# Moving a kernel's stores to a table among its score products, and two more warming products

## Chip, cores and metric

The kernel runs on one core of one Trainium2 chip. The metric is the device time of one execution in microseconds (us), the median of several runs. TensorE (PE) does the matrix products, VectorE (DVE), ScalarE (ACT) and GpSimd (POOL) the rest; SyncE (SP) issues most transfers, GpSimd the indirect ones.

## The reference, cut to what matters

```
scores = q @ k.T / 8                        # B = 8, H = 8, S = 576, D = 64, causal
scores += minimum(-(cum[i] - cum[j]), 0)    # cum: running sum of max(s, 0)
x[b, s, h*64:] = softmax(scores) @ v        # 4608 tokens of 512 numbers
logits = x @ w_gate                         # 8 experts
gate = sigmoid(x @ w_local)
e = argmax(logits) if first or gate < 0.5 else the expert of the token before
out = softmax(logits)[e] * (relu(x @ w1[e]) @ w2[e])
```

Everything is float32. A product in float32 is two records of each kind (weight load and product) in the trace.

## The kernel before, in words

**Attention.** The 64 heads are 32 pairs; the two heads of a pair use the two halves of TensorE's rows or columns at once. A *slot* m = 0 to 15 handles pairs n = 2m (even) and 2m + 1 (odd), and four slots' pairs cover two batch rows, a *group* g. In a slot TensorE first computes the score products of both pairs (`ps`, L874, 24 records a pair), in four units u = 0 to 3 for each pair. ACT exponentiates each unit into a tile e0 to e3 (L875), and POOL sets what lies above the diagonal to zero (the *masks*, L860: one each for e0, e1 and e2, two for e3). Then come the value products of the even pair and of the odd (`po`, L904, 100 records a pair), each in two parts of six and three blocks of 64 queries. The first blocks read the masked part of e0, the third block the masked part of e2, the fifth that of e3. DVE takes reciprocals (`recs`, L911) and writes the normalised tokens to `xb` (L912).

**Routing.** After each group the router computes logits of its 1152 tokens (`lp`, L216), the chosen experts, ranks within the expert (`pos`, L300 and L301), table rows (L309 to L316) and gates (up to L335). Then the group's tokens are stored to a `table` in DRAM, sorted by expert, in 18 stores of 64 tokens (128 half rows). One store (`put`) is two instructions on POOL, which runs its queue in order: a tiny write to `gap`, either a memset (L345) or a copy from a tile whose completion it thereby waits for (L347), and the indirect DMA (L348).

**Places.** The order on the engines is written out by hand. `plan(m, p, f)` puts work f at place p of slot m: 0 after the even pair's scores, 1 after the odd pair's, 3 and 4 after the even and odd values, 5 at the end of the slot. Since each engine takes its own instructions in this order, a store at place 0 stands on POOL behind the even pair's five masks, and one at place 1 behind the odd pair's. `STORES[g]` lists, from slot m + 2 on, the places at which a group's stores are issued; `m` is 4, 8 and 12. Stores at places 3, 4 and 5 copy an element of `recs`, so that they wait for the values named; the others don't wait. What `STORES` has no place for goes to `experts.puts`. The fourth group's stores all come later.

**Experts.** Tokens are handled in units of up to 256 rows of one expert. A unit's first layer is eight column blocks c = 0 to 7 (`hp`, L582, into `hT`, L584), its second layer `yp` (L606), whose result goes out by an indirect store (L611). In the first unit the loop takes one entry of `experts.puts` after each block, released by `hT` of that block; after block c = 2 the logits of the last group's second half are computed. When the list is empty in the first unit, rows of units 2 and 3 are fetched from the table by SP.

**Start.** Before the first score product TensorE multiplies zeros (`warm`, L809), while q and k arrive.

Of the kernel before, what the change touches and what calls it, by code (L numbers as in the profile page):

```python
# [45 lines left out]
NV = 4  # L46
NVA = 6
WEIGHED = (3, 7, 9, 11, 11, 13, 15, 19, 19, 21, 23, 27, 27, 30, 31, 31)
STORES = (((5,), (0, 1, 3, 4, 5), (0, 1, 3, 4, 5), (0, 1, 3, 4, 5), (0, 0)), ((5, 5), (0, 1, 3, 4, 5), (0, 1, 3, 4, 5), (0, 1, 1, 3, 4, 5)),
          ((5, 5), (0, 0, 1, 1, 3, 4, 5, 5)))  # L50
BX = 3
FIRST = ((0, P, 0, 3 * P), (P, S, 3 * P, S))
CAP = N + DH
# [399 lines left out]
class Experts:  # L453
# [165 lines left out]
    def run(self, recs, wend, out_of):  # L619
        tc, ctx, nc, router = self.tc, self.ctx, self.nc, self.router  # L620

        def pool(name, bufs, **kw):
            return ctx.enter_context(tc.tile_pool(name=name, bufs=bufs, reuse_waits="tile", **kw))

        self.w_rest = pool("w_rest", PLACES - 2)
        self.fp = pool("fp", 2)
        self.yp = pool("yp", 3)
        self.ps_h = pool("ps_h", 3, space=PSUM)
        self.ps_m = pool("ps_m2", 2, space=PSUM)
        self.ps_y = pool("ps_y", 2, space=PSUM)  # L630
        last, first = NG - 1, sum(EARLY)
        self.banks = lambda name: self.ps_m.tile([P, 1, 512], F32, name=name, tag="m")

        def late_rows():
            router.ranks(last, self.banks)
            router.rows(last)
            router.gates(last, self.xb)
            self.puts += [lambda after, c=c: router.scatter(last, c, after) for c in range(NC)]
            self.puts += router.pads()

        todo = {
            (0, 0): [lambda: self.load(0, 1, behind=self.hT[0][0:1, 0, 0:1]), lambda: self.load(1), lambda: router.assign_early(1), lambda: self.load(2)],
            (0, 2): [lambda: router.product(last, self.xts_of, self.banks, (1,)),
                     lambda: router.logits(last, (1,)), lambda: router.codes(last), lambda: router.exps(last),
                     lambda: router.turn1(last), lambda: router.turn2(last)],
            (0, "y"): [late_rows],
            (1, 2): [router.assign_doubles],
            (1, 5): [router.assign_rest],
            (2, 5): [lambda: in_range(tc, recs, wend, router.over, out_of, self.ps_m, router.ones)],
        }  # L650

        def at(u, c):
            for f in todo.pop((u, c), ()):
                f()

        before = {}
        for l in self.owner:
            for m in self.owner:
                if m < l and self.place(m) == self.place(l):
                    before[l] = m  # L660
        two = [m for m in self.owner if self.place(m) == "w_rest"]
        for i, l in enumerate(two):
            before[l] = two[i - 2] if i >= 2 else None
        self.turn_x(1)
        loaded, done, fetched, freed = [3, 3], (set(), set()), 2, False

        def ready(l, layer):
            nonlocal freed
            if before.get(l) is not None and self.owner[before[l]] not in done[layer]:
                return False  # L670
            if self.place(l) == "w_last" and not freed:
                if self.puts or todo:
                    return False
                self.x_stack.close()
                self.w_last = pool("w_last", 1, side="right")
                freed = True
            return True

        def loads():
            more = True  # L680
            while more:
                more = False
                for layer in range(2):
                    l = loaded[layer]
                    if l in self.owner and (not layer or l < loaded[0]) and ready(l, layer):
                        self.load(l, layer)
                        loaded[layer] += 1
                        more = True

        def fetches(u):  # L690
            nonlocal fetched
            while fetched <= u:
                self.fetch(fetched)
                fetched += 1

        def between(u):
            if self.puts:
                self.puts.pop(0)(None)
            at(u, "y")

        kinds = [k for k, _, _ in self.units]
        order = []
        u = 0
        while u < len(kinds):
            if u + 1 < len(kinds) and kinds[u + 1] in "MT":
                order += [(1, u), (1, u + 1), (2, u), (2, u + 1)]
                u += 2
            else:
                order += [(1, u), (2, u)]
                u += 1  # L710
        wanted = 0
        for what, u in order:
            last_wanted = wanted
            if what == 1:
                for c in range(FK):
                    self.layer1(u, c)
                    at(u, c)
                    if self.puts:
                        self.puts.pop(0)(self.hT[u][0:1, c, 0:1])
                    if u == 0 and fetched == 2 and not self.puts:  # L720
                        fetches(3)
                self.xT.pop(u)
                self.turn_h(u)
                if u:
                    self.turn_x(u + 1)
            else:
                self.layer2(u, lambda: between(u))
            done[what - 1].add(u)
            loads()
            if what == 1 and u and (u + 3 < first or not (self.puts or todo)):  # L730
                wanted = u + 3
            fetches(last_wanted)
        assert not todo and not self.puts


def attention(ctx, tc, q, k, v, s, wx, ident, recs, wend, router, experts):
# [69 lines left out]
    def warm_up(n):  # L806
        warm = banks("warm")[:, 0]
        for i in range(n):
            mm(warm[:, :P], lhsT=zero, rhs=zero, start=True, stop=True)  # L809

    warm_up(6)

    nc.vector.tensor_scalar(s_sb, s_sb, 0.0, None, Alu.max)
    nc.vector.tensor_tensor_scan(cum, ones, s_sb, 0.0, op0=Alu.mult, op1=Alu.add)
# [122 lines left out]
    for g in range(NG - 1):  # L937
        m = HP * GB // 2 * (g + 1)
        plan(m, 1, lambda g=g: router.product(g, of(g), banks))
        plan(m, 3, lambda g=g: router.logits(g))  # L940
        plan(m, 5, lambda g=g: (router.codes(g), router.turn1(g)))
        plan(m + 1, 1, lambda g=g: router.exps(g))
        plan(m + 1, 3, lambda g=g: router.turn2(g))
        plan(m + 2, 1, lambda g=g: router.ranks(g, banks))
        plan(m + 2, 3, lambda g=g: router.rows(g))
        plan(m + 2, 3, lambda g=g: router.gates(g, [xs[b] for b in range(g * GB, g * GB + GB)]))
        places = [(m + 2 + i, p) for i, ps in enumerate(STORES[g]) for p in ps]
        for c in range(NC):
            if c >= len(places):
                experts.puts.append(lambda after, g=g, c=c: router.scatter(g, c, after))  # L950
                continue
            i, p = places[c]
            after = {3: (2 * i, NJA), 4: (2 * i + 1, 0), 5: (2 * i + 1, NJA)}.get(p)
            after = after and recs[0:1, after[0], after[1], 0:1]
            plan(i, p, lambda g=g, c=c, after=after: router.scatter(g, c, after))
    m = NPAIR // 2
    plan(1, 5, router.constants)
# [10 lines left out]
    def at(slot, place):  # L968
        for f in todo.pop((slot, place), ()):
            f()  # L970

    for m in range(NPAIR // 2):
        pair = 2 * m, 2 * m + 1
        for n in pair:
            for u in range(len(UNITS)):
                if (n, u) == (0, 2):
                    key_exps()
                scores(n, u)
                if (n, u) == (0, 3):
                    key_weights()  # L980
                    weigh(0)
                    weigh(1)
                if (n % 2, u) == (1, 1):
                    load_v(n - 1 + NVA, es[n][u][0:1, 0, 0:1])
                    load_v(n + NVA)
            at(m, n - 2 * m)
        for n in pair:
            values(n, 0, NJA)[0]()
            evacuate, done = values(n, NJA, NJ)
            if n % 2 == 0:  # L990
                load_qk(n + NV, done)
                load_qk(n + 1 + NV)
            evacuate()
            at(m, 3 + n - 2 * m)
        last = m % HP == HP - 1
        if last:
            turns(pair)
        for n in range(WEIGHED[m - 1] + 1 if m else 2, WEIGHED[m] + 1):
            weigh(n)
        if not last:  # L1000
            turns(pair)
        at(m, 5)
# [575 lines left out]
```

## Time and profile before

| | us |
|---|---|
| median of 3 plain runs (734.1 to 735.39) | 734.65 |
| the profiled execution's own time | 753.2 |
| its span, first to last instruction | 751.5 |
| TensorE busy | 733.7 |
| POOL busy | 207.0 |
| value stage of a slot without stores (200 records) | 5.98 |
| score stage of a slot (48 records) | 5.76 |
| a store's indirect DMA on POOL, 54 of them, mean | 1.01 |

The profile lists each engine's busy time, the chain of work that ended last in order of time (start, length, what), groups of instructions by line, and for single stretches a timeline. A line of the timeline gives start, length, engine, line, operation, output and input, count, and in brackets how long the engine had been idle and what ended it. PEld is TensorE's weight load, which runs beside the products. "issue" is time in which an engine waited for nothing that the profile shows. Slot 7 begins at 94.95 us in the span, slot 11 at 149.98, slot 15 at 206.34, the first unit at 223.53.

### The profile page before, as it was taken

How to read it: one execution, taken by the hardware profiler on the slowest of the kernel's cores; microseconds unless marked ns; L12 is line 12 of the kernel's file. 1: busy time of each engine (PE TensorE's matmuls, PEld its weight loads, DVE VectorE, ACT ScalarE, POOL GpSimd, SP SyncE). 2: the span in 40 equal slices, each digit the busy share in tenths (PEclk: the TensorE clock that was granted, in tenths of full speed). 3: DMA queues.
4: the chain of work that ended last, by engine and by line, in shares of the span. 5: the costliest groups of instructions: out<-in, count | busy, mean ns of one | idle time of the engine just before them, and what ended most of it. 6: DMA issues, size and time to landing. Idle time of an engine off the chain costs nothing.

```text
span 751.5 us, 16161 instructions
## 1 busy us (share of the span) xinstructions
PE 733.7 (98%) x6517; PEld 502.5 (67%) x6517; DVE 253.2 (34%) x684; ACT 166.4 (22%) x355; POOL 207.0 (28%) x453
## 2 busy tenths in 40 slices
PE   9999999999989999999999999999999999999996
PEld 6888877878877567567657375537645676637674
DVE  4656668677756462101100511040132001050110
ACT  4545555355331011011001010101110111101110
POOL 3443367577575254340100001010101001000110
PEclk9999999999999999999999999999999999999998
DMA  8454464665639997698546979996999955899100
GB/s 280 165 176 159 142 199 150 199 214 170 187 88 363 356 397 221 235 425 211 229 145 204 375 235 423 303 388 255 427 309 381 426 193 228 283 386 359 36 15 32
DMA packets 57204, 187.28 MB, mean 249 GB/s; under 512 B 11869, under 2 KB 32093, under 8 KB 49568
## 3 DMA queue, kind: packets, MB, share of 16 engines
q1 hardware_dynamic: 50224, 165.91, 62.6%
q0 software_dynamic: 6800, 20.09, 7.0%
q8 instruction: 53, 0.87, 0.5%
q14 instruction: 31, 0.25, 0.1%
q10 hardware_dynamic: 96, 0.15, 0.1%
HBM read 165.50 MB, written 20.88 MB: 248 GB/s over the span
## 4 chain that ended last, share of the span: by engine, by line
PE 96%; issue 1%; DVE 1%; POOL 1%; DMA 1%; ACT 0%; SPq 0%; POOLq 0%; ACTq 0%
PE yp L606 34%; PE hp L582 31%; PE po L904 13%; PE ps L874 12%; PE hp L573 4%; PE lp L216 2%; DMA qb<-in_q_dram 1%; POOL table L348 0%; ACT e L875 0%; PE pos L300 0%; POOL e L860 0%; PE pos L301 0%; DVE xb L912 0%; SPq L769 0%; DVE y L609 0%
## 5 line engine op out<-in xcount | busy, mean ns | idle before, releaser
L606 PE MATMUL yp<-w2b,hT 128*128 128x512 f32 (+2 forms) x752 | 259.3, 593 | 0.0
L582 PE MATMUL hp<-xT,w1b 128*128 128x256 f32 (+1 forms) x1216 | 234.1, 353 | 0.0
L582 PEld LDWEIGHTS hp<-xT,w1b 128*128 128x128 f32 x1216 | 206.8, 191 | 32.9 <-issue 7.8
L606 PEld LDWEIGHTS yp<-w2b,hT 128*128 128x128 f32 (+2 forms) x752 | 107.9, 167 | 141.0 <-issue 139.6
L611 POOL DMA_INDIRECT out_dram<-y,gi x37 | 36.5, 986 | 416.8 <-DVE y L609 397.8
L584 ACT ACTIVATE hT<-hp 128x256 f32<-128x256 f32 (+1 forms) x152 | 54.0, 355 | 434.0 <-PE hp L582 420.8
L609 DVE TENSOR_SCALAR y<-yp,gi 128x512 f32<-128x512 f32 x37 | 27.6, 747 | 307.6 <-PE yp L606 307.6
L904 PE MATMUL po<-vg,e 128*64 128x66 f32 x3200 | 104.9, 223 | 7.0 <-issue 5.6
L875 ACT ACTIVATE e<-ps 128x768 f32<-128x768 f32 (+1 forms) x128 | 97.1, 837 | 47.1 <-PE ps L874 46.4
L904 PEld LDWEIGHTS po<-vg,e 128*64 128x64 f32 x3200 | 98.7, 138 | 13.0 <-issue 10.9
L874 PE MATMUL ps<-qb,kb 64*128 64x192 f32 (+4 forms) x768 | 98.1, 406 | 0.9 <-DMA qb<-in_q_dram 0.5
L874 PEld LDWEIGHTS ps<-qb,kb 64*128 64x128 f32 x768 | 66.2, 190 | 31.8 <-ACT e L875 15.2
L860 POOL TENSOR_SCALAR_AFFINE_SELECT e<-e 128x256 f32<-128x256 f32 (+1 forms) x160 | 67.3, 445 | 51.9 <-ACT e L875 50.8
L348 POOL DMA_INDIRECT table<-xb,idx x54 | 54.5, 1010 | 19.5 <-issue 17.2
L593 DVE STREAM_TRANSPOSE hT<-hs 32x256 f32<-32x256 f32 x64 | 27.9, 436 | 74.8 <-ACT hs L575 74.0
L854 DVE TENSOR_TENSOR vg<-va,wk 128x256 f32<-128x256 f32 x64 | 41.4, 711 | 0.0
L911 DVE RECIPROCAL recs<-po 128x12 f32<-128x12 f32 x64 | 13.5, 211 | 64.4 <-PE po L904 47.9
L552 DVE STREAM_TRANSPOSE xT<-xq 128x1024 f32<-128x1024 f32 (+1 forms) x23 | 23.7, 1028 | 16.5 <-DMA xq<-table 15.9
L573 PE MATMUL hp<-w1b,xT 128*32 128x512 f32 (+1 forms) x224 | 28.3, 594 | 0.0
L912 DVE TENSOR_TENSOR xb<-po,recs 128x384 f32<-128x384 f32 (+1 forms) x48 | 22.0, 458 | 1.9 <-POOL e L860 0.3
L573 PEld LDWEIGHTS hp<-w1b,xT 128*32 128x32 f32 (+1 forms) x224 | 8.1, 114 | 17.7 <-issue 17.6
L923 DVE STREAM_TRANSPOSE xt<-xb 128x576 f32<-128x576 f32 x24 | 17.1, 751 | 0.0
(229 smaller groups left out, 195.5 us busy)
## 6 DMA issues: line engine op xcount, KB each, us to landing
w2b<-in_w_dram SPq DMA_DIRECT2D x30, 2048.0 KB
w1b<-in_w_dram SPq DMA_DIRECT2D x29, 2048.0 KB
va<-in_v_dram SPq DMA_DIRECT2D x32, 320.0 KB
kb<-in_k_dram SPq DMA_DIRECT2D x31, 288.0 KB
qb<-in_q_dram SPq DMA_DIRECT2D x31, 288.0 KB
xq<-table SPq DMA_DIRECT2D x56, 130.0 KB
w1b<-in_w_dram SPq DMA_DIRECT2D x4, 512.0 KB
xq<-table SPq DMA_DIRECT2D x20, 65.0 KB
```

The costliest lines, as they stand in the source:

```text
L348: put = self.nc.gpsimd.indirect_dma_start(out=self.halves, in_=src, element_offset=0, in_offset=None, out_offset=bass.IndirectOffsetOnAxis ...
L573: mm(ps[d, :], lhsT=xT[:, k, d], rhs=self.ws[l][0][:, k, c * 512 : c * 512 + 512], start=(k == 0), stop=(k == DK - 1))
L582: mm(ps[:, :w], lhsT=self.ws[ls[0]][0][:, k, c * P : c * P + P], rhs=xT[:, k, :w], start=(k == 0), stop=(k == DK - 1))
L584: nc.scalar.activation(self.hT[u][:, c, :w], ps[:, :w], Act.Relu)
L593: self.nc.vector.transpose(hT[32 * a : 32 * a + 32, :, 32 * r : 32 * r + 32], hs[32 * r : 32 * r + 32].rearrange("p (c i) -> p c i", i=P)[ ...
L606: mm(ps[d, :], lhsT=hT[:, k, n * P + d.start : n * P + d.stop], rhs=self.ws[l][1][:, k, :], start=(k == 0), stop=(k == FK - 1))
L611: put = nc.gpsimd.indirect_dma_start(out=self.out[:, :], out_offset=bass.IndirectOffsetOnAxis(ap=gi.bitcast(I32)[:, n, 0:1], axis=0), in_= ...
L854: nc.vector.tensor_tensor(vg[:, to].rearrange("p c h e -> p (c h) e")[:, :, :DH], va[:, :c].rearrange("p c h e -> p (c h) e"), wk[:, n, to ...
L860: nc.gpsimd.affine_select(out=ap, in_=ap, compare_op=Alu.is_ge, fill=0.0, base=base, pattern=n, channel_multiplier=-1)
L874: mm(ps[:, h, at : at + z - a], lhsT=kb[d, key : key + P], rhs=qb[d, a:z], start=True, stop=True)
L875: nc.scalar.activation(e, ps, Act.Exp, scale=scale)
L904: mm(po[d, j - j0, :], lhsT=weights_of(n, c, j, h), rhs=vgs[n % NV][:, c if j < 2 * G1 else G1 + c, h, :], start=(c == 0), stop=(c == last))
```

## The change

`STORES` is written anew. Places 3 and 4 are no longer used; a new place 2 lies after unit u = 1 of the even pair's scores, so that a store there stands on POOL between the even pair's second and third masks. Place 5 takes two stores in most slots. The number of stores in the attention goes from 46 to 43 (slots 6 to 15), and `experts.puts` has 11 entries in place of 8 when the first unit begins. There they are taken one after blocks 0, 1 and 3, none after block 2, and two after each of blocks 4 to 7; other units take one a block as before. The warming products are eight in place of six.

```diff
-STORES = (((5,), (0, 1, 3, 4, 5), (0, 1, 3, 4, 5), (0, 1, 3, 4, 5), (0, 0)), ((5, 5), (0, 1, 3, 4, 5), (0, 1, 3, 4, 5), (0, 1, 1, 3, 4, 5)),
-          ((5, 5), (0, 0, 1, 1, 3, 4, 5, 5)))
+STORES = (((5, 5), (2, 0, 1, 5, 5), (2, 0, 5, 5), (2, 0, 5, 5), (2, 0, 0)), ((5, 5), (2, 0, 1, 5, 5), (2, 0, 1, 5, 5), (2, 0, 0, 5, 5), (2,)),
+          ((5, 5), (2, 0, 0, 5, 5)))
...
-                    if self.puts:
-                        self.puts.pop(0)(self.hT[u][0:1, c, 0:1])
+                    for _ in range((1, 1, 0, 1, 2, 2, 2, 2)[c] if u == 0 else 1):
+                        if self.puts:
+                            self.puts.pop(0)(self.hT[u][0:1, c, 0:1])
...
-    warm_up(6)
+    warm_up(8)
...
-            after = {3: (2 * i, NJA), 4: (2 * i + 1, 0), 5: (2 * i + 1, NJA)}.get(p)
-            after = after and recs[0:1, after[0], after[1], 0:1]
+            after = recs[0:1, 2 * i + 1, NJA, 0:1] if p == 5 else None
...
+                if (n % 2, u) == (0, 1):
+                    at(m, 2)
```

## Prediction

> **What bounds the kernel now.** I read the busy times first, then the chain that ended last, then the timeline of single stages.
>
> ```profile
> PE 733.7 (98%) x6517; PEld 502.5 (67%) x6517; DVE 253.2 (34%) x684; ACT 166.4 (22%) x355; POOL 207.0 (28%) x453
> L904 PE MATMUL po<-vg,e 128*64 128x66 f32 x3200 | 104.9, 223 | 7.0 <-issue 5.6
> L348 POOL DMA_INDIRECT table<-xb,idx x54 | 54.5, 1010 | 19.5 <-issue 17.2
> ```
>
> TensorE holds the end. GpSimd (POOL) has 28% over the span, but its stores lie in slots 6 to 15, where a store holds it for about 1.0 us. The chain shows one stage without stores and one with:
>
> ```profile
> 89.04 5.98 PE po L904 x200
> 95.02 5.76 PE ps L874 x48
> 100.78 1.60 PE po L904 x49
> 102.38 0.10 issue
> 102.49 2.82 PE po L904 x89
> 105.31 0.15 issue
> 105.46 0.32 PE po L904 x3
> 105.78 0.42 issue
> 106.19 0.39 PE po L904 x6
> 106.59 0.35 issue
> 106.94 1.76 PE po L904 x53
> 108.70 5.88 PE ps L874 x48
> ```
>
> 200 value products take 5.98 us undisturbed (slot 6) and 7.92 in slot 7, with gaps that no semaphore explains. They follow the ends of stores (102.18, 105.10, 106.45). An isolated store costs the products 0.37 us (slot 8: two stores, 6.75 for 5.98), the second of two back to back about 1.15 (slot 7). Over slots 7 to 15 the value stages lose 1.94, 0.77, 0.78, 0.95, 2.73, 0.85, 1.92, 0 and 3.99: 13.9 us. Score stages lose 1.5 together. The first unit's 64 logit products take 4.79 us where slot 15 needs 1.46; [...]:
>
> ```profile
> 228.90:233.69 4.79, 2.92 (x65) 2.18 (x64) 1.33 (x8) 0.38 (x1) 2.05 (x3) 0.83 0.97 378
> 233.69:243.31 9.62, 9.62 (x42) 8.36 (x41) 7.51 (x35) 1.74 (x5) 4.01 (x8) 0.91 1.00 424
> ```
>
> (columns: length, then busy time of PE, weight loads, DVE, ACT and POOL, then the clock, 0.83 and 0.91). That is 3.3 + 1.0, and 0.2 before it: 4.5 us. The second limit is POOL's order. It masks the exponentials that the values read; slot 11:
>
> ```profile
> 152.57 1.47 POOL L348 DMA_INDIRECT table<-xb,idx  x1 [0.58 <-POOL gap L347]
> 154.42 0.98 POOL L348 DMA_INDIRECT table<-xb,idx  x1 [0.16 <-issue]
> 155.42 1.72 POOL L860 TENSOR_SCALAR_AFFINE_SELECT e<-e 128x256 f32<-128x256 f32 x5
> 155.88 0.43 PEld L904 LDWEIGHTS po<-vg,e 128*64 128x64 f32 x12 [0.21 <-POOL e L860]
> 156.59 1.82 PEld L904 LDWEIGHTS po<-vg,e 128*64 128x64 f32 x59 [0.27 <-POOL e L860]
> ```
>
> Two place-5 stores held the masks until 155.42; TensorE waited for them twice, 0.48 us.
>
> **Profile against plain runs.** The profiled execution took 753.2 (span 751.5, 1.7 around it), the plain median is 734.65: 18.55 less. Cross every stall off the profiled span: 13.9 + 1.5 + 4.5, and 1.1 in value stages of slots 0 to 2, leave 751.5 - 21.0 = 730.5, with the outside 732.2. Plain runs stand only 2.4 above that, 11% of the 21. From unit 1 on the products run at a constant step (64 hp records in 13.81, 32 yp in 13.73), so no other stage can hide 18 us. Small products may run a little faster unprofiled: a pair of value records takes 59.8 ns, the line through hp and yp (0.833 ns a column and 2.5) gives 57.5 for 66 columns. Over 1600 pairs that is 3.7 us, and then 30% may remain (38% if nothing lay around the span). So I take the gaps after stores to be mostly a cost of being recorded, while mask waits are ordinary semaphore waits and stay.
>
> [...] 128-column products 213 ns apart at the start, 0.53 of the clock in 232.0 to 235.6. [...] POOL's 0.98 us a store is engine time that delays what is queued behind.
>
> **The change, part by part.** POOL prices from slots 7 and 11: first store of a group 1.44 after a gap copy; the next starts 0.35 after an end; store 0.98; masks step 0.36, the last 0.24; first mask ends 0.43 after a store; a store behind masks starts 0.2 after them. Times below are from the first score product of the slot. The values of the even pair need mask e0 at once, e2 0.36 after their start, e3 0.60 later; the odd pair the same, 2.99 after.
>
> *Slot 7.* Before: one place-5 store to 4.23, masks to 6.05, values from 5.76, no wait. After: a second place-5 store to 5.6; e0 6.0, e1 6.35; place 2 puts a store here, to 7.5; e2 7.95, e3 8.55. Values start at 6.05, stand at 6.4 until 8.0: 0.3 + 1.6 = **1.9 us** new wait.
>
> *Slot 11.* Place 5 twice as before (e1 ends 6.2); place 2 store to 7.4; e2 7.8 instead of 6.55: **1.25**.
>
> *Slots 10, 13, 15.* Two place-0 stores now stand before the odd masks, and place 2 has delayed the even ones. Slot 10: place-5 stores to 4.4 (reciprocals late, as at 1.69 and 3.22 before), place 2 to 6.4, even masks to 7.4, stores to 9.9, odd e0 10.35 against 9.46 needed, e2 another 0.35 late: 1.2. Slot 13 likewise 0.95, slot 15 1.3. Sum 3.45. Any gap that remains after the paired stores delays the need as well, and 0.3 us of slack in POOL takes each away: I count two thirds, **2.3** (bounds 0 and 3.45).
>
> *Slots 8, 9, 12, 14.* Place 2 ends its masks by 6.5 to 8.0, and values start at 5.8 to 8.1 behind logits (2.31) or ranks (0.71): nothing, covered by these; at most 0.3 each. The store of slot 14 is also the last reader of the buffer that DVE writes at 8.65 (202.53); it is issued by 6.5, so its landing is in time unless it takes over 2.1.
>
> *Stores leaving the values.* Places 3 and 4 go. But place 0 lands 0.7 to 1.7 us into the values, since POOL trails ACT, and place 1 3 to 4 us in. Remaining loss as profiled: slots 7 and 11 two isolated each (0.74), 8, 9, 12 one (0.37), 10, 13, 15 a pair (1.52): 7.15, against 13.9 - 0.48 of masks = 13.4; 6.3 saved. Score stages: as much as before, place-5 pairs come to more slots.
>
> *First unit.* No store issues at c = 2; the one of c = 1 still ends just inside the logits. I keep 1.0 of the 4.5: 3.5 saved as profiled. Eleven stores in place of eight, two per column block from c = 4: 2.6 us of POOL per 1.73, so it ends some 4 us later. Next on POOL is the first output store, which comes 7.6 us into layer 2; fetches 2 and 3 on SP wait for those stores and go 4 us later, as do weight loads queued behind; the turn of unit 2 (274.3, before its products at 285) covers them. Nothing, at most 0.3.
>
> *Warming.* Two products are four records of 213 ns: 0.85, in front of a wait for q that ends at 6.35 anyway; they fill the idle 3.85 to 4.55. Delay 0.15, hidden. [...] I take 0.4.
>
> *Sum.* Stores: 6.3 + 3.5 = 9.8 as profiled; 11% of it in plain runs, 1.1 (bounds 0 and 3.7). Plain: 1.9 + 1.25 + 2.3 - 1.1 - 0.4 = +4.0: 734.65 + 4.0 = **738.6**. The profiled execution goes the other way: pairs hide the waits of 10, 13 and 15, so 753.2 - 9.8 + 3.2 - 0.4, about 746.
>
> **Rivals.** *Faster.* The gaps after stores are real in plain runs up to the 30 to 38% that the floor allows. Place: slots 10, 13, 15 and the first unit. Price: 3.7 saved, which also hides the waits of the paired slots, clock 1.3, masks 3.15 and no more: 732.8; with the slot 7 wait smaller, 731. For it: every gap follows a store, and the first unit's clock drop is on record. Against: the floor of 732.2. It decides once stores save more than masks cost, from about a third remaining. *No difference.* POOL is quicker behind place 2 (masks of e2 in time, as in slot 9) so that slot 7 and 11 cost 1 to 1.5: 734.6. *The edit doesn't do what it says.* Two stores per slot still lie in values; this is in the sum. *Slower yet.* All waits count (6.6 + 0.3 to 0.9 elsewhere, nothing saved): 741.7.
>
> **How the numbers follow.** Waits win, 70%, own range 736.3 to 741.5; rival faster 18%; no difference 12%. Within 0.2% (1.5 us) is about what a measurement of this kernel cannot tell from no change. The range 732.0 to 742.0 takes in the bound with all waits and most of the faster case.
>
> **What would show it.** In the profile after: waits of po for POOL e grow from 1.1 us to 4 or more; slot 7's even values stand about 1.6 us after their first 12 records; e2's mask follows a store; no gaps late in the values of slots 8 and 9; 64 logit products in the first unit near 2 us at full clock; full clock at or before 10.2 us. I am wrong if po doesn't wait for POOL in slots 7 and 11, or if the plain median falls while the profiled span falls by as much.

## The result and the profile after

The changed kernel took 741.19 us (median of 6 runs, 740.46 to 741.93), the kernel before 734.49 beside it (733.61 to 735.39): ratio 1.0091, 95% interval 1.0078 to 1.0104. It is slower by 6.7 us, where 4.0 had been forecast.

The sets of experiments ran on different chips (10, 7, 3 and 4 in the record), all runs of a set on the same one, and the very same kernel before takes 734 to 735 us in some (the result's runs, sets 3 and 4 below) and 751 to 752 in others (sets 1 and 2), so every figure is read against the kernel before of its own set.

The profile after was taken in an execution of 741.93 us, with a span of 740.2. The lines that answer to those of before, from the busy times and the groups:

```profile
PE 724.7 (98%) x6521; PEld 498.4 (67%) x6521; DVE 250.8 (34%) x684; ACT 165.9 (22%) x355; POOL 204.7 (28%) x453
L905 PE MATMUL po<-vg,e 128*64 128x66 f32 x3200 | 100.5, 223 | 7.1 <-POOL e L861 5.3 <-issue 1.3
L348 POOL DMA_INDIRECT table<-xb,idx x54 | 55.5, 1028 | 17.0 <-issue 15.0 <-POOL gap L347 1.2 <-ACT hT L584 0.7
```

The idle time of the value products is as large as before, 7.1 for 7.0 us, but its cause has changed: it was "issue", and is now POOL's masks. PE is busy for 9.0 us less than in the profile of before, 4.4 of it in the value products: their standstills behind stores were in part counted as busy there. In this profile no value stage stands still at "issue" behind a store; the 1.3 us of "issue" left lie in slots 0 and 2, which have no stores. The waits of the weight loads (us in total, times, longest) say the same; they had been 1.1 in 5 times:

```profile
PEld po L905 <- POOL e L861: 7.8, 14, 1.5
```

The chain (start, length, what) through slot 7, which begins at 94.54:

```profile
97.33 1.44 POOL table L348
99.13 0.98 POOL table L348
100.12 0.77 POOL e L861 x2
101.09 0.98 POOL table L348
102.09 0.42 POOL e L861
102.56 5.70 PE po L905 x188
108.26 5.88 PE ps L875 x48
```

Two stores from place 5, two masks, the store at place 2, the third mask; then 188 value products in one piece, although two more stores end while they run (at 104.27 and 107.18). The value stage waited 0.29 for its first mask and 1.62 for the third. In slot 10, which begins at 134.63, the chain goes further back, to DVE:

```profile
135.41 0.56 DVE xb L913
136.11 0.37 DVE xb L913
136.50 0.33 POOL gap L347
137.21 1.19 POOL table L348
138.41 0.23 POOL gap L347
138.80 0.98 POOL table L348
139.80 0.77 POOL e L861 x2
140.76 0.98 POOL table L348
141.75 0.43 POOL e L861
142.23 2.81 PE po L905 x88
```

The first unit has no gap left. Its logit products take what slot 15's take, and the layer behind them has a clock of 1.00 (columns: length, busy times of PE, weight loads, DVE, ACT and POOL, clock, DMA share, GB/s):

```profile
221.91:223.37 1.46, 1.46 (x66) 1.31 (x65) 1.23 (x8) 0.38 (x1) 0.99 (x1) 1.00 0.91 359
223.37:232.11 8.74, 8.74 (x45) 7.71 (x42) 7.62 (x37) 1.70 (x5) 3.81 (x8) 1.00 1.02 429
```

So the two profiles read as if two things had happened: gaps of some 18 us gone, and waits for masks of some 7 us come. The experiments show that the first was not the change's doing.

### The profile page after: what moved, and what is told of

The parts are those of the page before. It is cut to its first block, busy times and chain, and to the rows that moved or that the text cites. A ratio compares the mean times of both kernels' runs of the same rounds, so it can differ in the third digit from the quotient of the medians.

```text
span 740.2 us, 16154 instructions
## 1 busy us (share of the span) xinstructions
PE 724.7 (98%) x6521; PEld 498.4 (67%) x6521; DVE 250.8 (34%) x684; ACT 165.9 (22%) x355; POOL 204.7 (28%) x453
## 4 chain that ended last, share of the span: by engine, by line
PE 89%; POOL 5%; DVE 2%; issue 1%; ACT 1%; DMA 0%; SPq 0%; POOLq 0%
PE yp L606 35%; PE hp L582 31%; PE po L905 10%; PE ps L875 8%; PE hp L573 4%; POOL table L348 3%; POOL e L861 1%; PE lp L216 1%; DVE xb L913 1%; PE warm L810 1%; DMA qb<-in_q_dram 0%; ACT e L876 0%; DVE recs L912 0%; POOL gap L347 0%; DVE l L231 0%
## 5 line engine op out<-in xcount | busy, mean ns | idle before, releaser
L905 PE MATMUL po<-vg,e 128*64 128x66 f32 x3200 | 100.5, 223 | 7.1 <-POOL e L861 5.3
L905 PEld LDWEIGHTS po<-vg,e 128*64 128x64 f32 x3200 | 96.2, 138 | 11.2 <-POOL e L861 7.8
L875 PE MATMUL ps<-qb,kb 64*128 64x192 f32 (+4 forms) x768 | 94.5, 399 | 0.3 <-ACT e L876 0.3
L861 POOL TENSOR_SCALAR_AFFINE_SELECT e<-e 128x256 f32<-128x256 f32 (+1 forms) x160 | 64.0, 425 | 50.8 <-ACT e L876 49.7
L855 DVE TENSOR_TENSOR vg<-va,wk 128x256 f32<-128x256 f32 x64 | 39.9, 689 | 0.0
```

The costliest lines, as they stand in the source:

```text
L855: nc.vector.tensor_tensor(vg[:, to].rearrange("p c h e -> p (c h) e")[:, :, :DH], va[:, :c].rearrange("p c h e -> p (c h) e"), wk[:, n, to ...
L861: nc.gpsimd.affine_select(out=ap, in_=ap, compare_op=Alu.is_ge, fill=0.0, base=base, pattern=n, channel_multiplier=-1)
L875: mm(ps[:, h, at : at + z - a], lhsT=kb[d, key : key + P], rhs=qb[d, a:z], start=True, stop=True)
L905: mm(po[d, j - j0, :], lhsT=weights_of(n, c, j, h), rhs=vgs[n % NV][:, c if j < 2 * G1 else G1 + c, h, :], start=(c == 0), stop=(c == last))
```

## The experiments

The theory after the result: waits for masks, made by POOL's order, cost the 6.7 us; the gaps behind stores in the profile of before are absent from the runs compared. The rival: recording puts the gaps in. A second rival: the order of stores doesn't matter, only that more of them come late. Below, "excess" is the length of a value stage, from its first value product, over 5.98 us, summed over slots 7 to 15 in the profile of the kernel named. It holds gaps and waits for masks alike; a wait ahead of the first product, as the 0.29 of slot 7, is not in it.

### Set 1 (kernel before in it: 751.93, 748.97 to 754.05)

**The kernel before, unchanged.**

> The kernel before, unchanged, profiled once more. If the gaps behind stores belong to one recorded execution and not to the kernel, this profile has value stages of 5.98 us with stores in them, a span near 733 us, and POOL waits of about half a us in slot 11 alone. If the gaps belong to stores beside values, they are there again: 7.9 us in slot 7, 10.0 in slot 15, span near 751.

The one profiled execution took 751.02; its span was 749.3. Its excess is 13.17 us, and the first unit's logits take 4.15, for 13.9 and 4.79 in the profile that the prediction used. But the plain runs of this set take just as long. The gaps are thus no cost of being recorded: here plain runs are as long as the profile with gaps, and among the result's runs the profiled one has none.

**No store at place 2** (but in slot 14):

```diff
-STORES = (((5, 5), (2, 0, 1, 5, 5), (2, 0, 5, 5), (2, 0, 5, 5), (2, 0, 0)), ...
+STORES = (((5, 5), (1, 0, 1, 5, 5), (1, 0, 5, 5), (1, 0, 5, 5), (1, 0, 0)), ...
```

> The changed kernel with every place-2 store moved to place 1 (behind the odd pair's masks), except the one of slot 14. POOL-order theory: the even masks come 1.25 us earlier, the waits of slots 9, 11 and 12 vanish, slot 7 keeps 0.6, slots 10 and 13 about 0.6 each, slot 15 next to none; 8.7 us of waits become about 2, time near 734.6. Rival (stores beside score products, the first unit's burst or the warming cost the time): the place-5 and place-0 stores, the burst and the products are all still there, so the time stays near 741, at best 740.

748.72 us, ratio 0.9966 (0.9953 to 0.9978). Both expectations, 734.6 and 741, were for a kernel before of 734, so the time can't decide between them. The excess is 13.84, that of the changed kernel in set 2 13.33. Weight loads of the values wait 1.5 us for masks where the changed kernel has 5.5 there, and stand 11.4 us at "issue" for 6.7: what the masks no longer cost, the stores now cost by lying among the values.

**One store at place 0 instead of two** in slots 10, 13 and 15:

```diff
-(2, 0, 0)   ...   (2, 0, 0, 5, 5)
+(2, 0, 1)   ...   (2, 0, 1, 5, 5)
```

> The changed kernel with the second place-0 store of slots 10, 13 and 15 moved to place 1; place 2 stays. POOL-order theory: the odd masks of these slots come 1.3 us earlier; slot 10 falls from 2.0 to 0.7 us of waiting, slot 13 from 1.9 to 0.3, slot 15 from 1.4 to 0.1; time near 737.1. Rival: three stores of 43 are moved and stay beside values, nothing changes: 741.

744.92 us, ratio 0.9920 (0.9904 to 0.9937), the best of these two sets: 7.0 us below its kernel before, where the changed kernel is 2.7 below its own in set 2 (none ran in this set). The excess is 9.80; slots 10, 13 and 15 have 1.45, 0.74 and 0.49 where the changed kernel has 2.14, 1.72 and 1.48 in set 2. The pair at place 0 costs 0.7 to 1.0 in each, masks and gaps together.

**Eight warming products alone** (`warm_up(8)` in the kernel before):

> The kernel before with eight warming products in place of six. Forecast: 0.4 us faster [...], between 0 and 1.7 faster. Rival: the products delay the first scores by 0.15 to 0.3 us and the time is the same or that much longer.

750.94 us, ratio 0.9987 (0.9971 to 1.0003). Between a gain of 2 us and nothing; not resolved.

### Set 2 (kernel before in it: 751.45, 748.05 to 754.87)

**The changed kernel, unchanged.**

> The changed kernel, unchanged, beside the others. Where the kernel before takes about 734 us: 741 again, with waits for masks of 8.7 us in the value stages. Where it takes about 752 because of gaps behind stores: the waits remain in slots 7, 9 and 11, those of slots 10, 13 and 15 hide behind gaps; before's gaps of 21 us fall to some 12; about 746. If masks were not the cost, it would be slower than before in both.

748.75 us, ratio 0.9969 (0.9957 to 0.9981). Here the same change makes the kernel faster, by 2.7 us; about 746 had been expected. Slot 7 in its chain has the wait for masks and two standstills after it:

```profile
99.22 0.77 POOL e L861 x2
100.19 0.98 POOL table L348
101.18 0.43 POOL e L861
101.65 1.96 PE po L905 x59
103.69 2.77 PE po L905 x80
106.61 1.67 PE po L905 x49
```

The pieces of values end where a store ends (103.37 and 106.28 on POOL, the products stand soon after): 188 products take 6.6 us here, where 5.70 were enough in the profile after. In the profiles the gain lies mainly in the first unit: its logits take 2.92 us here and the rest of the layer 8.74, where set 1's kernel before has 4.15 and 10.42, 2.9 us together. The attention's excess is 13.33 against 13.17: gaps left the values and waits for masks took their place, at par. The weight loads' idle time shows both, in set 1's kernel before (first two lines) and here:

```profile
PEld po L904 <- issue: 9.3, 29, 0.5
PEld po L904 <- POOL e L860: 1.1, 5, 0.3
PEld po L905 <- issue: 6.7, 21, 0.6
PEld po L905 <- POOL e L861: 5.5, 8, 1.5
```

**Both undone together** (place 2 to 1 and the second place 0 to 1):

> The changed kernel with its place-2 stores moved to place 1 (but slot 14's) and the second place-0 store of slots 10, 13 and 15 moved to place 1 too. POOL-order theory: only slot 7 keeps 0.6 us of waiting and slot 10 about 0.3; where before takes 734, about 733.5; where it takes 752, the stores at place 1 bring gaps in the values, about 745 to 747. Rival (stores beside score products are dear): as slow as the changed kernel.

748.45 us, ratio 0.9955 (0.9941 to 0.9969), excess 13.78. 745 to 747 had been expected; it is hardly better than the changed kernel. The waits for masks are down to 1.0 us, but all its stores in slots 7 to 15, save those of places 0 and 5 and slot 14's, now stand behind the odd masks, and "issue" is up to 11.4. This kernel comes again in set 4.

**All the attention's stores among the values:**

```diff
-STORES = (((5,), (0, 1, 3, 4, 5), ...
+STORES = (((4,), (1, 1, 3, 3, 4), ...
```

with nothing at places 0 and 5 in any slot.

> The kernel before with all its stores in the attention at places 1, 3 and 4, thus behind the odd masks and beside value products, none ahead of a mask. POOL-order theory: no value product waits for a mask; where before takes 734, the same or 0.5 us faster. Gap theory: where before takes 752, five stores a slot now stand in values with back-to-back pairs; 3 to 8 us slower than before.

768.34 us, ratio 1.0233 (1.0201 to 1.0265): 16.9 us slower, twice and more the 3 to 8 that were expected. The value stage of slot 8 takes 9.48, slot 12 10.72 and slot 15 12.07 for 5.98. Its chain in slot 8:

```profile
117.58 2.13 PE po L904 x67
119.78 0.38 PE po L904 x5
120.15 0.39 issue
120.54 0.44 PE po L904 x6
120.98 0.31 issue
```

The profile shows no semaphore that is waited for; "issue" twice, with six products between. In this set, where a store lies decides 17 us.

**First unit's stores away from the logits**, in the kernel before: none after block 2, two after block 7.

```diff
+for _ in range((1, 1, 0, 1, 1, 1, 1, 2)[c] if u == 0 else 1):
```

> The kernel before with no store released by block 2 of the first unit (beside its logits) and two by block 7. Gap theory: where before takes 752, the 64 logit products fall from 4.2 us to about 2.7 and the clock is not halved behind them (1.7): 3 us faster. Where before takes 734 nothing: there the logit products were not slowed.

749.25 us, ratio 0.9975 (0.9964 to 0.9987): 2.2 us from this part alone, of 2.7 for the whole change in the same set; 3 had been expected. The layer behind the logits takes 8.74, as in the profile after and in the changed kernel of this set, where its clock is 1.00; the logits still take 3.59, and not 2.7.

### Set 3 (kernel before in it: 734.84)

**Work on POOL in slots 3 to 6, which have no stores** (core of the edit; `probe` writes `gap2` and does the work named). Theory A puts the gaps down to an indirect transfer, whatever its bytes, B to the bytes moving, C to any busy instruction on POOL:

```diff
+for i, kind in ((3, "small"), (4, "work"), (5, "store"), (6, "plain")):
+    plan(i, 1, lambda kind=kind: router.probe(kind, 0, ident[0:1, 0:1]))
+    plan(i, 3, lambda kind=kind, i=i: router.probe(kind, 1, recs[0:1, 2 * i, NJA, 0:1]))
```

> The kernel before with two pieces of work on POOL added to each of the slots 3 to 6, whose value stages have no store and take 5.98 us: one behind the slot's masks (place 1), one released by the even pair's reciprocals, so in the odd values (place 3). Slot 3: an indirect store of the same 128 rows but 32 bytes each, into a table of its own that nobody reads; slot 4: five memsets, about 1 us of POOL, no transfer; slot 5: an indirect store of 128 rows of 1040 bytes, as the real ones, into a table of its own; slot 6: the same bytes by a plain transfer that ACT issues. The results are not touched. Theory A [...]: slots 3 and 5 grow by 0.6 to 1.1 us each, slots 4 and 6 stay at 5.98. Theory B (they come from the bytes moving): slots 5 and 6 grow, slot 3 little, slot 4 nothing. Theory C [...]: slots 3 to 6 all grow. If the kernel before takes about 734 in this comparison, the slots 7 to 15 should show no gaps behind stores, and then none of the four slots grows under A and B. Time: A +1 to +2 us where the kernel before takes about 752, nothing where it takes about 734.

734.93 us, ratio 1.0001 (0.9991 to 1.0012). The value stages of slots 3 to 6, and slot 7 with its real stores (columns as above):

```profile
51.41:57.39 5.98, 5.98 (x202) 5.91 (x201) 2.14 (x6) 1.68 (x4) 3.69 (x8) 1.00 0.74 214
65.46:71.44 5.98, 5.98 (x204) 5.92 (x200) 3.21 (x14) 0.15 (x1) 2.03 (x11) 1.00 0.40 128
77.21:83.19 5.98, 5.98 (x202) 5.91 (x201) 3.73 (x16) 2.00 (x6) 3.50 (x8) 1.00 0.62 186
89.67:95.65 5.98, 5.98 (x201) 5.91 (x201) 3.20 (x13) 1.17 (x5) 1.69 (x9) 1.00 0.67 199
101.41:107.39 5.98, 5.98 (x202) 5.91 (x200) 2.38 (x7) 1.83 (x6) 5.33 (x14) 1.00 0.70 192
```

Nothing grows: neither by added work nor in slot 7, three of whose stores end in its values and cost 1.94 us in the profile of before. As this chip shows no gap behind any store, the run doesn't tell the theories A, B and C apart. It shows that POOL's time and the bytes by themselves cost TensorE nothing here: 5.98 in each of the five stages.

**One store at the ends of slots 6, 10 and 14**, in the changed kernel:

```diff
+STORES = (((5,), (2, 0, 1, 5, 5), (2, 0, 1, 5, 5), (2, 0, 5, 5), (2, 0, 1)),
+          ((5,), (2, 0, 1, 5, 5), (2, 0, 1, 5, 5), (2, 0, 1, 5, 5), (2, 0)), ((5,), (2, 0, 1, 5, 5)))
```

> The changed kernel with one store in place of two at the end of slots 6, 10 and 14, and the second place-0 store of slots 10 and 13 at place 1 (slot 8 and slot 15 take one more store at place 0 or 1, the first unit one more after its block 3). The masks of slot 7 then end 1.4 us sooner (e0 at about 4.6 after the slot's start, e2 at 6.6), those of slots 11 and 15 by 1.3, and the odd masks of slots 10, 13 and 15 stand behind one store less. Theory (waits for masks are what the change costs, gaps behind stores are what it gains, and how large the gaps are differs with where the kernel runs): where the kernel before takes about 734, this takes 735 to 736.5, against 741 for the changed kernel; where it takes about 752, the gaps in slot 7 hide part of what is saved, and it takes 744 to 746, against 748.75 for the changed kernel. Rival (the masks don't matter, stores beside values do): the same as the changed kernel in either place, 741 or 748 to 749, since as many stores stay beside values.

739.39 us, ratio 1.0079 (1.0059 to 1.0099): between the two expectations for such a chip and nearer the rival's. By stages, slot 7 loses 0.65 for 1.9, slots 10, 13 and 15 0.67, 0.66 and 0 for 2.0, 1.9 and 1.4. But slot 14, which had lost 0.08, loses 3.25. The chain there:

```profile
191.68 1.01 POOL e L861 x3
192.88 3.09 DMA table<-xb,idx
196.46 0.56 DVE xb L913
197.16 3.14 PE po L905 x100
```

The edit put a store at place 0 of slot 14, the last reader of the buffer of tokens that DVE fills next. DVE waited 2.76 us for it to land, so value sums stayed in their buffers, and TensorE waited 2.2 us for DVE. The mistake was the experiment's; taking off those 3.2 us leaves 736.2, an estimate that lies within what the theory expected.

### Set 4 (kernel before in it: 734.37)

**Both undone together, again.**

> The changed kernel with its place-2 stores at place 1 (but for slot 14) and the second place-0 store of slots 10, 13 and 15 at place 1, once more: as many stores as the changed kernel has in the attention, at the same ends of slots, but none that stands on POOL ahead of masks that the values are waiting for, save the pairs at place 5. Theory (the loss of 6.7 is waits for masks): where the kernel before takes about 734, slot 7 keeps 0.3 of its 1.9, slot 11 0.3 of 0.6, slots 10, 13 and 15 next to nothing of 5.3; 733.5 to 735.5, within 0.2% of the kernel before. Where that one takes about 752, 748 to 749 as it did there. Rival (the order of the stores doesn't matter, only that more of them are late, pairs at place 5, or the longer first unit): 740 to 741 where the kernel before takes about 734.

735.40 us, ratio 1.0011 (1.0005 to 1.0018). It has as many stores in the attention as the changed kernel, the same pairs at place 5, the same first unit and eight warming products; only the place-2 stores (but slot 14's) and the second one at place 0 of a slot went behind the odd masks. The loss to the kernel before is 1.0 us in place of 6.7, and the waits for masks are 2.8 us in place of 7.8:

```profile
PEld po L905 <- POOL e L861: 2.8, 8, 1.0
```

This speaks for the masks and against the second rival: as many stores come late, in pairs and in the first unit as in the changed kernel. The excess is 2.24, where the same kernel had 13.78 in set 2: 11.5 us of gaps in one program, in one set and not in the other. Against what was expected, slot 9 (0.46; 0.62 in the next kernel, without the change in the attention) and slot 14 (1.04) remain. Slot 14 has the one place-2 store left:

```profile
190.10 0.98 POOL table L348
191.11 0.42 POOL e L861
191.57 5.70 PE po L905 x188
```

**Warming and first unit alone**, in the kernel before (`warm_up(8)` and the tuple of blocks above):

> The kernel before with two parts of the change alone, those that put nothing on POOL ahead of a mask: eight warming products, and in the first unit no store after block 2 but two after block 7 (eight in all, as before). Theory: where the kernel before takes about 734 there is no gap in the first unit to win back, and the warming starts the values up to 1.4 us sooner of which a part is given back in slot 0: 733 to 734.5. Where it takes about 752, the two gains that were seen alone there add up, 2.2 and 0.6 to 1: 748 to 749.5. In both it is then at or below both kernels. Rival (warming is given back whole, the first unit is luck): the same as the kernel before in both.

734.28 us, ratio 0.9998 (0.9990 to 1.0006): no gain where the first unit has no gap. Its chain through slot 7 is that of the prediction with the gaps taken out:

```profile
93.05 5.76 PE ps L875 x48
98.81 5.98 PE po L905 x200
104.80 5.88 PE ps L875 x48
```

Its excess is 1.69. Where there are no gaps, the stores of the kernel before cost next to nothing where they are, and no version run there is measurably faster than it.

## Why the prediction was right, and where it failed

The side was right, the size 2.6 us too small, at the upper edge of the prediction's own range; the rival "slower yet", with all waits counted and nothing saved, gave 741.7, which is near to what came. The terms, against the excess of the kernel with warming and first unit alone (no gaps, same warming):

| step | forecast | measured |
|---|---|---|
| slot 7, place-5 pair and place 2 | +1.9 | 0.29 + 1.62 = +1.9 |
| slot 11 | +1.25 | 0.59 - 0.36 = +0.2 |
| slots 10, 13, 15 | 3.45, counted as +2.3 | 5.33 - 0.56 = +4.8 |
| slots 8, 9, 12, 14 | 0 | 0.85 - 0.75 = +0.1 |
| stores leaving values and logits | -1.1 | 0 |
| warming | -0.4 | not resolved: set 4's kernel with it 0.1 below the one before |
| sum | +4.0 | +7.0 by the stages, +6.7 by the medians |

**The waits of slot 7** came as worked out from POOL's queue: masks were forecast to end at 6.0, 6.35, 7.95 and 8.55 after the slot's start and ended at 6.00, 6.35, 7.96 and 8.55.

**Slots 10 and 13 were mis-sized by reading a store for another.** I let the place-5 stores of slot 10 begin at 1.69 after the slot's start, as in the profile of before. But the store at 1.69 is place 4's of slot 9, which waits for the odd pair's first reciprocals (128x12). Place 5's waits for the last ones (128x6), 0.72 later, and it came second, at 3.22. Slot 10 of before begins at 136.58:

```profile
137.24 0.21 DVE L911 RECIPROCAL recs<-po 128x12 f32<-128x12 f32 x1
137.96 0.18 DVE L911 RECIPROCAL recs<-po 128x6 f32<-128x6 f32 x1
138.27 0.98 POOL L348 DMA_INDIRECT table<-w2b,idx  x1 [0.51 <-DVE recs L911]
139.80 0.99 POOL L348 DMA_INDIRECT table<-w2b,idx  x1 [0.16 <-issue]
```

After, both stores are place 5's. The first came at 2.58, the pair ended at 5.16 and not at 4.4, and the masks and stores behind it came 0.65 to 0.75 later than worked out: 2.0 us of waits for 1.2. DVE itself was not later (last reciprocals 1.44 after the slot's start, 1.56 before). In slot 13 the first store went from 0.69, again place 4's, to 2.02; there DVE is later too, by 0.63, since slot 12 became shorter (15.25 to 14.30) and the router's work on DVE did not.

**Slot 11 was mis-sized the other way**, by times from a stage that the change stretches. The place-5 stores ahead of its masks wait for reciprocals behind the router's work on DVE. Slot 10 became 1.07 longer (13.40 to 14.47), DVE's work did not (the first store came 15.9 us after the start of slot 10, before 16.0), and so that store came at 1.42 after the start of slot 11 and not at 2.59. The two errors nearly cancel: for slots 7, 10, 11, 13 and 15 the prediction has 6.6 before it counts two thirds, the runs 6.9. That this sum, and with it the 741.7, came out so close is luck.

**"I count two thirds"** failed too: it let gaps that remain hide the waits. No gap remained in the runs compared, so all of it showed: 1.15 us of what was missing, with 1.1 more from the stores' savings that did not come.

**"The gaps after stores are mostly a cost of being recorded"** was the right subtraction for a wrong reason. The arithmetic held: crossed off, they left 732.2, and kernels before without gaps take 734.3 to 734.9. The 2.4 between, which I took for the 11% of gaps that remain, are nearly all losses that are there without gaps: the kernel with added work of set 3 has 1.38 us in the value stages of slots 7 to 15 (waits for masks in slot 11 and for DVE in slot 13 among them) and 0.7 in those of slots 0 to 2, 2.1 together. So the store savings were not 1.1 but nothing. But recording doesn't make the gaps: plain runs of sets 1 and 2 are as long as their profiles, and the profile after has none. That the profile of before came from a chip with gaps, and the plain times shown beside it from one without, is what the sets suggest; it is not shown, for the chips of these runs are not known.

**"The profiled execution goes the other way, about 746"** failed in the comparison: the profiled execution took 741.93, like the others. In set 2, where there are gaps, the change brought 2.7 and not the 7 forecast (-9.8 + 3.2 - 0.4). The first unit gave 2.9 of 3.5. In the attention 6.3 saved and 3.2 lost had been forecast; the excess stayed where it was (13.33 for 13.17), with weight loads at "issue" for 2.6 us less and waiting for masks for 4.4 more. Gaps did not hide the waits of slots 7 and 10 (excess 2.54 and 2.14). Score stages, forecast to lose as much as before, lost 0.2 in set 2 for 1.0 in set 1's kernel before.

**The rival "faster"** is right where gaps are in plain runs: there the change is faster, and the first unit, one of the places it names, gives most of it. Of its other places, slots 10, 13 and 15, only slot 15 gains much (1.49 for 3.68). Its evidence, a clock of 0.83 during the first unit's logits and of 0.91 in the layer behind them, stands in the profile of before (1.00 in both in the profile after); the floor that spoke against it holds where there are no gaps.

**Place 2 behind logits and ranks costs nothing:** right in the changed kernel (slots 8, 12 and 14: 0, 0.25 and 0.08), but not in general: in the kernel of set 4 slot 13 is 1.92 shorter, the first store of slot 14 comes at 2.51 after its start and not at 1.56, and the values behind the ranks wait 1.0 us for the mask behind the place-2 store.

**The 0.4 for warming, and the 1.3 for the clock in the rival "faster",** were estimates of mine that no median here shows. In the profiles a 448-column score record lasts 536 ns on the mean after (6.9 to 7.7 us) and 949 before (7.7 to 9.2), and the first value product begins at 13.05 after and at 14.44 before; slot 7 begins 0.41 sooner.

**The first unit's eleven stores cost nothing later:** right; from the end of its first layer the profile after has 501.4 us to the last product (232.11 to 733.51), and that of before 501.4 (243.31 to 744.71), as every other profile here has.

## What to carry to other kernels

Before a stall is given a price, see whether it is in the runs that are compared: here an own time of the profiled execution 2.5% above the plain median was no cost of recording, but the sign of a profile that shows another condition. When an instruction is moved on an in-order queue, write out what that queue then delays, with the release that each instruction waits for, in times of the engine that gives it and not in times from a stage that the change itself shortens or stretches. In the sets without gaps, a queue off the critical path with 28% load carried stores for next to nothing behind the last mask that TensorE waited for (in set 4's kernel with warming and first unit alone, an excess of 1.69 us over nine stages), and cost up to 2 us a stage with stores ahead of it.

## What the runs showed of the hardware

- The same program takes 734.4 to 734.8 us on two chips (4 and 3) and 751.5 to 751.9 on two others (7 and 10). No chip was used in two of the four sets, so whether the chip makes the difference, or something else about the time of a set, is not shown. In the profiles the difference is mainly standstills of TensorE around the ends of indirect stores, 11.5 us in the attention for one kernel that ran in both conditions, and the first unit: in set 1's kernel before its logits take 4.15 us and the rest of the layer 10.42, in the profile after 1.46 and 8.74. POOL itself is not slower: its stores take 1010 ns on the mean in set 1's kernel before and 1005 in set 4's, which has the same stores. In these standstills the profile shows no semaphore that TensorE waits for: weight loads of the values stand at "issue" for 9.3 us in set 1's kernel before and for 6.7 in set 2's changed kernel. What makes them is open: the run with work added on POOL met none, with 5.98 us in each of slots 3 to 7.
- A store's interval on POOL is not its landing. In slot 14 of the kernel with one store at the ends of slots, POOL was done 0.98 us after 192.88, and the transfer took 3.09; DVE, which needed the buffer, waited 2.76 us and went on at 196.46.
